# Attention, gated mixer and a Strassen-type MLP on one core: other pieces converted ahead, second tokens taken backwards

## The chip, the core and the metric

One NeuronCore of a Trainium2 chip runs the whole program. The metric is device time in microseconds (us) from the first to the last instruction and what lies around it, as the median of several runs. The kernel works in float32; matmuls take their operands as pairs of a high and a low part (`fp32r`), three matmuls for each product.

## The reference

Four sequences of 576 tokens go through attention (half of the heads local, half strided), then a gated mixer, then an MLP with a norm ahead of it. The change lies in the MLP:

```python
def _moe2_ref(x, g_ln, w_ch1, w_ch2):
    mu = np.mean(x, axis=-1, keepdims=True)
    var = np.mean((x - mu) ** 2, axis=-1, keepdims=True)
    xn = (x - mu) / np.sqrt(var + 1e-06) * g_ln
    ch = np.maximum(xn @ w_ch1, 0.0) @ w_ch2
    return (x + ch).astype(np.float32)
```

Here `x` has 4 x 576 x 512 values, `w_ch1` 512 x 2048, `w_ch2` 2048 x 512. Both weights arrive as 64-bit floats.

## The kernel before

**Stages.** Up to about 292 us attention and mixer run, batch after batch. Behind them stands `last_stage`, the MLP over three sets of 768 tokens (`sc` 0, 1, 2). `NW` is 8: the 2048 hidden units are eight *pairs* of two blocks of 128. A pair (`pair` for the first tokens, `joint_pair` for the second and third) multiplies by the scheme of Strassen and Winograd: seven products (`product`, L979, six matmuls each) in place of eight, with sums of weights and of inputs made ahead. For the first tokens the second product follows in plain form (`ch2`, L247 to L249). For the second and third tokens the second product is itself of the Strassen kind over the two sets: `step2` (L1197) with *slices* of `w_ch2` (M1 to M7) and *grains*, the inputs split in two parts (`grain`).

**Pieces of weights.** `wseq` counts pieces (i, j): j = 0, 1 are the two pieces of the first-product weight of pair i, j = 2, 3 those of the second-product weight. A raw piece is loaded as 64-bit numbers (512 KB, L784) into one of two raw buffers in `stg`, taken in turn, and turned into float32 by `from_f64` (one ScalarE instruction, L232; two of VectorE, L235 and L236). Ten pieces, listed in `PRE`, are converted in spare time before 292 us by `pre_w` in twenty halves and written to the scratch `w_d`; `piece` then loads them ready (256 KB, L779). `third` gives the float32 place of a second-product piece: two places in `stg`, one in the tile `late`. First-product pieces go to `stg2`.

`combine(i)` makes four sums in VectorE (L796 to L799), then splits all into the weight tile `w` of pair i (L760 on ScalarE, L761 on VectorE, or L218 and L219). `split_later` leaves the VectorE half to the next `flush`. `keep(i)` stores `w` to `w1_d` (L805); `fetch(i)` loads it again for later tokens (L814). There are two tiles for `w`, for even and odd i. `second(i)` splits the second-product pieces, and `store_f32` writes their float32 form to `w2_d` (L772), from where the slices come later.

**Order.** The first-token loop does `pair(0, i)`, then `prepare(6)`: six units of the list `units`, in which after pair i come the second weight of i + 1, `combine(i + 2)`, then the second-product pieces of i + 2, then the first-product pieces of i + 3. So `w` of pair i + 2 is made after pair i, and its pieces one pair earlier. All transfers go out from SyncE in one queue, which waits in order. A planner lays out each engine's order within what the data allows; `add_manual_dep` with `ORDER` fixes one instruction behind another.

**Second and third tokens.** `joint` runs pairs 0 to 7 of the second tokens, then M1 and M2 with i from 0 to 7, then pairs 0 to 7 of the third tokens, then M7, M6, M5, M4, M3. Weights 0 and 1 are fetched ahead of each set of pairs, and weight i + 2 after pair i. `sums_of(e)` makes four sums of blocks of `w_ch2` (L1136 to L1139), `store_sums` stores them, `sum_slices(m, places)` loads a sum and splits it for Mm. `rsqrt` makes the reciprocal root of the norm, half of the tokens at a time.

## Time and profile before

| what | us |
|---|---|
| median of 3 runs | 675.0 |
| lowest and highest run | 674.49, 679.81 |
| the profiled execution, whole | 677.46 |
| its span, first to last instruction | 675.5 |
| TensorE busy in the span | 651.6 |
| VectorE busy | 521.9 |
| ScalarE busy | 398.5 |

The granted clock of TensorE is 0.992 over the span, that is 2.4 GHz nearly throughout. In the profile PE is TensorE (PEld its weight loads), DVE VectorE, ACT ScalarE, POOL GpSimd and SP SyncE; L979 is line 979 of the kernel before. An idle time in brackets stands with the instruction that ended it and names what it had waited for. A tile's name is cut at its number (`w1b` stands for `w1b_0` and `w1b_1`), and every scratch tensor of weights is called `w_scratch`. TensorE's busy time overlaps from one matmul to the next; a pause can also be a missing record, and then no releaser stands behind it.

### The profile page before, as it was taken

To read this page: it belongs to the slowest core of one execution; us is meant where nothing else is said; L and a number is where in the kernel's file an instruction comes from. 1 tells how busy PE (TensorE), PEld (TensorE's weight loads), DVE (VectorE), ACT (ScalarE), POOL (GpSimd) and SP (SyncE) were. 2 spreads that over 40 slices of the span, in tenths; PEclk is the share of its full clock that TensorE was granted. 3 is DMA by queue.
4 is the path that set the end of the run, shared out by engine and by line. 5 is a ranking of instruction groups with operands and counts; after the bars stand their busy time and mean duration, and the time that the engine had idled before them with its cause. 6 is when DMAs were issued, how large, how long until landed. Compare 5 with 4: busy or idle time off the path is not lost.

```text
span 675.5 us, 12971 instructions
## 1 busy us (share of the span) xinstructions
PE 651.6 (96%) x4958; PEld 620.9 (92%) x4958; DVE 521.9 (77%) x997; ACT 398.5 (59%) x908; POOL 19.3 (3%) x24
## 2 busy tenths in 40 slices
PE   8989999999999999999999799999999999999997
PEld 6778989988897988999999699989999999999997
DVE  6878887585668688997699894585695774799893
ACT  5868967283458547645458863357874454856540
POOL 0021011000110011000000000000000000000000
PEclk9979999998999999999999999999999999999999
DMA  8772333457443470439978886498883797322234
GB/s 317 240 256 76 117 117 116 156 161 220 137 140 98 160 238 4 172 140 330 379 260 332 289 304 197 128 343 321 269 287 130 232 308 242 93 67 62 67 106 128
DMA packets 61453, 130.66 MB, mean 193 GB/s; under 512 B 5392, under 2 KB 28560, under 8 KB 60368
## 3 DMA queue, kind: packets, MB, share of 16 engines
q1 hardware_dynamic: 61392, 129.84, 57.6%
q8 instruction: 39, 0.64, 0.4%
q14 instruction: 22, 0.18, 0.1%
HBM read 94.69 MB, written 35.13 MB: 192 GB/s over the span
## 4 chain that ended last, share of the span: by engine, by line
PE 68%; DMA 10%; DVE 10%; ACT 8%; issue 2%; POOL 1%; SPq 0%; ACTq 0%; POOLq 0%; DVEq 0%
PE ps_p L979 18%; PE ps_m L1197 17%; PE ps_o L247 3%; PE ps_o L249 3%; PE ps_o L248 3%; DMA w_scratch<-w_p 2%; PE ps_y L249 2%; PE ps_y L247 2%; PE ps_y L248 2%; DMA stg<-in_w_ch 2%; PE ps_g L247 2%; PE ps_g L248 2%; PE ps_g L249 2%; PE ps_t L515 2%; PE ps_u L247 1%
## 5 line engine op out<-in xcount | busy, mean ns | idle before, releaser
L979 PE MATMUL ps_p<-x,w1b 128*128 128x384 f32 x672 | 120.6, 336 | 2.5 <-ACT u L1167 1.4
L979 PEld LDWEIGHTS ps_p<-x,w1b 128*128 128x128 f32 x672 | 116.1, 188 | 5.6 <-ACT u L1167 3.5
L1197 PE MATMUL ps_m<-t,w2c 128*128 128x384 f32 x420 | 74.1, 334 | 0.0
L1197 PEld LDWEIGHTS ps_m<-t,w2c 128*128 128x128 f32 x420 | 72.9, 188 | 0.0
L979 PE MATMUL ps_p<-x,w 128*128 128x384 f32 x336 | 63.5, 338 | 2.2 <-DVE w L219 1.3
L979 PEld LDWEIGHTS ps_p<-x,w 128*128 128x128 f32 x336 | 58.0, 188 | 4.2 <-DVE w L219 1.7
L247 PE MATMUL ps_u<-xhl,winl 128*128 128x288 f32 x128 | 39.2, 306 | 2.6 <-ACT u L354 2.6
L247 PE MATMUL ps_g<-wsg,vn 128*128 128x288 f32 x128 | 39.0, 305 | 0.0
L249 PE MATMUL ps_u<-xhl,winh 128*128 128x288 f32 x128 | 38.9, 304 | 0.0
L248 PE MATMUL ps_u<-xhl,winh 128*128 128x288 f32 x128 | 38.9, 304 | 0.0
L249 PE MATMUL ps_g<-wsg,vn 128*128 128x288 f32 x128 | 38.3, 299 | 0.0
L249 PE MATMUL ps_y<-gt,wout 128*128 128x288 f32 x128 | 38.1, 299 | 0.0
L248 PE MATMUL ps_g<-wsg,vn 128*128 128x288 f32 x128 | 38.1, 297 | 0.0
L247 PE MATMUL ps_y<-gt,wout 128*128 128x288 f32 x128 | 37.7, 297 | 0.0
L248 PE MATMUL ps_y<-gt,wout 128*128 128x288 f32 x128 | 37.6, 296 | 0.0
L248 PE MATMUL ps_o<-h,w2x 128*128 128x384 f32 x96 | 32.2, 335 | 0.2 <-DVE h L992 0.2
L249 PE MATMUL ps_o<-h,w2x 128*128 128x384 f32 x96 | 32.1, 334 | 0.0
L247 PEld LDWEIGHTS ps_u<-xhl,winl 128*128 128x128 f32 x128 | 25.2, 197 | 3.1 <-ACT u L354 2.7
L635 POOL TENSOR_TENSOR rs<-ve,neghalf 128x1 f32<-128x1 f32 x20 | 19.1, 957 | 244.5 <-DVE ve L633 244.5
L248 PEld LDWEIGHTS ps_u<-xhl,winh 128*128 128x128 f32 x128 | 25.2, 197 | 0.2
L249 PEld LDWEIGHTS ps_u<-xhl,winh 128*128 128x128 f32 x128 | 25.1, 196 | 0.0
L247 PEld LDWEIGHTS ps_g<-wsg,vn 128*128 128x128 f32 x128 | 24.1, 188 | 0.6
(340 smaller groups left out, 1670.3 us busy)
## 6 DMA issues: line engine op xcount, KB each, us to landing
w1b<-w_scratch SPq DMA_DIRECT2D x32, 512.0 KB, 4.8
w_scratch<-w SPq DMA_DIRECT2D x8, 1792.0 KB, 7.5
w1b<-w_scratch SPq DMA_DIRECT2D x48, 256.0 KB, 4.7
stg<-in_w_ch SPq DMA_DIRECT2D x22, 512.0 KB, 5.1
raw_p<-in_w_ch SPq DMA_DIRECT2D x20, 256.0 KB, 3.2
blk<-w_scratch SPq DMA_DIRECT2D x10, 512.0 KB, 5.4
qk<-in_qk_s SPq DMA_DIRECT2D x8, 601.0 KB, 4.8
qk<-in_qk_l SPq DMA_DIRECT2D x8, 592.0 KB, 4.9
```

Source lines behind the costliest of these rows:

```text
L247: nc.tensor.matmul(ps, lhsT=ll, rhs=rh, start=first, stop=False)
L248: nc.tensor.matmul(ps, lhsT=lh, rhs=rl, start=False, stop=False)
L249: last_mm[0] = nc.tensor.matmul(ps, lhsT=lh, rhs=rh, start=False, stop=last)
L515: nc.tensor.transpose(ps[:rows, (t - t0) * c:(t - t0 + 1) * c], src, ident)
L635: nc.gpsimd.tensor_tensor(out=rs, in0=ve, in1=neghalf[:, :1], op=ALU.pow)
L979: nc.tensor.matmul(o, lhsT=w[:, n0 + nk * k, a, :], rhs=x[:, c, k, :], start=first and k == 0 and n == 0, stop=k == 1 and n == 2, skip_gro ...
L1197: nc.tensor.matmul(banks[e, half][:, :TH], lhsT=sl[m, e][a][:, i, :], rhs=g[:, c, half * TH:(half + 1) * TH], skip_group_check=True, start ...
```

## The change

- `PRE` names other pieces: (2,0) and (2,1) stay; (3,0) to (6,1) of the first product are replaced by (3,2), (3,3), (4,2), (4,3), (5,2), (5,3), (6,2), (6,3) of the second. `ready` gives their place: the second-product ones go straight to `w2_d`, and `second` no longer puts them on the list that `store_f32` stores.
- The first-product pieces of pairs 3 to 6 are therefore raw. `wide(i)` gives their float32 place: the first 1792 columns of the second `late` tile for i = 3 and 5, `stg2` for the others. The third place of `third` moves to the last 512 columns of that tile. A `flush` stands ahead of the conversion of (7,0).
- One tile for even and one for odd weights serves all passes (`w1_tile`). The second tokens go through pairs 7 to 0, and M1 and M2 with i from 7 to 0. The two fetches ahead of the second and those ahead of the third tokens go.
- The roots of the second tokens are made at f = 9 and 12 of the first tokens' second half, not at pairs 6 and 7 of the second tokens.
- `sums_of` is put behind the last add of a pair, for e = 0 after pair 3 of the order (before: 2); `store_sums` follows after pair 4 (before: 3), in another order of blocks.
- The slices for M7 come in two steps: e = 0 after pair 5 of the third tokens into the two `w2y` tiles, e = 1 behind the last pair's `u4` copy. M7 takes i = 0, 1, 2 for e = 0, then the same for e = 1, then the rest.

```diff
@@ -73,7 +73,7 @@
           (2, "u", 0), (2, "u", 1), (2, "u", 3), (2, "u", 4), (2, "u", 5), (2, "u", 6), (2, "u", 7))
-PRE = (8, 9, 12, 13, 16, 17, 20, 21, 24, 25)
+PRE = (8, 9, 14, 15, 18, 19, 22, 23, 26, 27)
 XH_ACT = ((0, 1, 2, 3), ())
@@ -728,6 +728,9 @@
 
+    def ready(i, j):
+        return w_d[PRE.index(wseq.index((i, j)))] if j < 2 else w2_d[i, :, (j - 2) * WP:(j - 1) * WP]
+
     raws, stores = [], []
@@ -738,7 +741,7 @@
             n, half, f = stores.pop(0)
-            nc.sync.dma_start(out=w_d[n, :, half * (WP // 2):(half + 1) * (WP // 2)], in_=f)
+            nc.sync.dma_start(out=ready(*wseq[PRE[n]])[:, half * (WP // 2):(half + 1) * (WP // 2)], in_=f)
         if len(raws) > 1 or m >= 2 * len(PRE):
@@ -748,10 +751,15 @@
 
+    def wide(i):
+        if i not in (3, 5):
+            return big["stg2"]
+        return big["late", 1].rearrange("p f t -> p (f t)")[:, :1792].bitcast(U32)
+
     def third(n):
...
         if k == 2:
-            return big["late", 1].rearrange("p f t -> p (f t)")[:, 2 * TH:2 * TH + WP].bitcast(U32)
+            return big["late", 1].rearrange("p f t -> p (f t)")[:, 1792:].bitcast(U32)
         return big["stg"][:, 2048 + WP * k:2048 + WP * (k + 1)]
@@ -773,10 +781,12 @@
         stg = big["stg"]
-        w = third(2 * i + j - 2) if j > 1 else big["stg2"][:, WP * j:WP * (j + 1)]
+        w = third(2 * i + j - 2) if j > 1 else wide(i)[:, WP * j:WP * (j + 1)]
         k = wseq.index((i, j))
         if k in PRE:
-            nc.sync.dma_start(out=w.bitcast(F32), in_=w_d[PRE.index(k)])
+            nc.sync.dma_start(out=w.bitcast(F32), in_=ready(i, j))
+            if j == 2:
+                store_f32()
         else:
@@ -784,11 +794,13 @@
                 store_f32()
+            if (i, j) == (NW - 1, 0):
+                flush()
             from_f64(raw, w, None, 2)
...
     def combine(i):
-        c = big["stg2"].bitcast(F32)
+        c = wide(i).bitcast(F32)
         wf = c[:, 0:1024].rearrange("p (k f) -> p k f", k=KD)
@@ -798,17 +810,19 @@
         flush()
-        w = w1[i] = big["w1", i % 2].tile([P, 14, 2, P], F32R, tag="w1", name=f"w1_{i % 2}")
+        w = w1[i] = w1_tile(i % 2)
         (split_later if 0 < i < NW - 1 else split)(w[:, :, 0], w[:, :, 1], c.rearrange("p (n f) -> p n f", f=P))
...
 
+    def w1_tile(j):
+        if ("w1t", j) not in big:
+            big["w1t", j] = big["w1", j].tile([P, 14, 2, P], F32R, tag="w1", name=f"w1_{j}")
+        return big["w1t", j]
+
     def fetch(i):
-        j = i % 2
-        if ("w1b", j) not in big:
-            big["w1b", j] = big["w1", j].tile([P, 14, 2, P], F32R, tag="w1", name=f"w1b_{j}")
-        w = w1[i] = big["w1b", j]
+        w = w1[i] = w1_tile(i % 2)
         src = w1_d[i].rearrange("p (n a f) -> p n a f", a=2, n=14)
@@ -829,7 +843,8 @@
             (split_later if i + 1 < NW else split)(w2[i][0][:, k], w2[i][1][:, k], f)
-            f32s.append((i, k, f))
+            if wseq.index((i, 2 + k)) not in PRE:
+                f32s.append((i, k, f))
 
@@ -1082,14 +1097,14 @@
             leave(0, 0, d)
-        fetch(0)
-        fetch(1)
         for f in range(NF):
...
                 residual(0, 1)
+            if f in (9, 12):
+                rsqrt(1, f // 12)
             ch2(0, 1, f, 0)
@@ -1130,21 +1145,21 @@
 
-    def sums_of(e):
+    def sums_of(e, last):
         tt = nc.vector.tensor_tensor
         a11, a21, a22, a12 = (blk[g] for g in range(4))
-        tt(out=a22, in0=a21, in1=a22, op=ALU.add)
+        op = tt(out=a22, in0=a21, in1=a22, op=ALU.add)
+        tc.add_manual_dep(op.ins, last.ins.name, ORDER, reason="pair first")
         tt(out=a21, in0=a11, in1=a21, op=ALU.subtract)
...
     def store_sums(e):
-        for g in (1, 2, 0, 3):
+        for g in (3, 1, 2, 0):
             nc.sync.dma_start(out=ws_d[g, e], in_=blk[g])
 
-    def sum_slices(m, places):
-        n = NW * P
-        for e in range(2):
+    def sum_slices(m, places, behind=None, es=(0, 1)):
+        for e in es:
             hi, lo = places[2 * e:2 * e + 2]
@@ -1152,7 +1167,10 @@
                 nc.sync.dma_start(out=sl[m, e][1].bitcast(F32), in_=w2_d[:, :, c0:c0 + P].rearrange("i p q -> p i q"))
-            split(hi, lo, lo.bitcast(F32))
+            op = nc.scalar.activation(hi, lo.bitcast(F32), AF.Copy)
+            if behind is not None:
+                tc.add_manual_dep(op.ins, behind.ins.name, ORDER, reason="pair first")
+            nc.vector.tensor_tensor(out=lo, in0=lo.bitcast(F32), in1=hi, op=ALU.subtract)
 
@@ -1161,6 +1179,8 @@
         return a
+
+    pair_op, copy_op = [None], [None]
 
@@ -1179,13 +1199,13 @@
         u4 = tmp("u4")
-        copy(u4, a)
+        copy_op[0] = copy(u4, a)
         tt(out=b[:, 1, TH:], in0=o, in1=u4, op=ALU.add)
...
         product(sc, i, o, 4, False)
-        tt(out=b[:, 1, :TH], in0=o, in1=u2, op=ALU.add)
+        pair_op[0] = tt(out=b[:, 1, :TH], in0=o, in1=u2, op=ALU.add)
         relu(b[:, 1, :], b[:, 1, :])
@@ -1196,7 +1216,8 @@
                                      rhs=g[:, c, half * TH:(half + 1) * TH], skip_group_check=True,
-                                     start=m in (1, 2, 7, 4) and i == 0 and k == 0, stop=i == NW - 1 and k == 2)
+                                     start=(m, i) in ((1, NW - 1), (2, NW - 1), (7, 0), (4, 0)) and k == 0,
+                                     stop=i == (0 if m < 3 else NW - 1) and k == 2)
 
@@ -1252,39 +1273,36 @@
 
-        a = begin_pair(1, 0)
+        a = begin_pair(1, NW - 1)
         for i in range(NW):
-            a = joint_pair(1, i, a, hv[1, i], lambda: begin_pair(1, i + 1) if i + 1 < NW else None)
+            u = NW - 1 - i
+            a = joint_pair(1, u, a, hv[1, u], lambda: begin_pair(1, u - 1) if u else None)
             if i == 0:
...
                     load_block(0, g, g)
-            if i == 3:
+            if i == 4:
                 store_sums(0)
-            if i + 2 < NW:
-                fetch(i + 2)
+            if u > 1:
+                fetch(u - 2)
             for step in NORM2_AT.get(i, ()):
                 norm(2, step, 0)
-            if i == 2:
-                sums_of(0)
-            if i >= NW - 2:
-                rsqrt(1, i + 2 - NW)
-        fetch(0)
-        fetch(1)
+            if i == 3:
+                sums_of(0, pair_op[0])
         acc = {}
...
             acc[eh] = pl.tile([P, 512], F32, tag=tag, name="ps_m1")
-        order = [(m, i) for m in (1, 2) for i in range(NW)]
+        order = [(m, i) for m in (1, 2) for i in range(NW - 1, -1, -1)]
         ring[2] = big["wst"].tile([P, 2 * TC], F32R, tag="stg2", name="gr_3")
...
         for n, (m, i) in enumerate(order):
-            if (m, i) == (1, 2):
+            if (m, i) == (1, NW - 3):
                 for g in range(3):
                     load_block(1, g, g)
-            if (m, i) == (2, 0):
+            if (m, i) == (2, NW - 1):
                 other = {eh: bank_d("ps_m2") for eh in EH}
@@ -1292,8 +1310,8 @@
                 make(*order[n + len(ring)])
-            if (m, i) in EXPAND2_AT:
-                expand(2, EXPAND2_AT[m, i])
+            if (m, NW - 1 - i) in EXPAND2_AT:
+                expand(2, EXPAND2_AT[m, NW - 1 - i])
         for e, half in EH:
@@ -1318,7 +1336,7 @@
             if i == 2:
-                sums_of(1)
+                sums_of(1, pair_op[0])
             if i == 3:
@@ -1326,11 +1344,16 @@
                 rsqrt(2, i - 1)
+            if i == 4:
+                y0, y1 = (big["w2p", b].tile([P, NW * P], F32R, tag="w2y", name="w2c") for b in range(2))
+                sets = {0: [y1, y0]}
+            if i == 5:
+                sum_slices(7, sets[0], pair_op[0], (0,))
             if i == NW - 2:
-                sets = {}
-                sets[0] = slice_set(0)
-                sum_slices(7, sets[0])
-        sets[1] = slice_set(1)
+                free = thirds(0)
+                sets[0] += free[:2]
+        sum_slices(7, sets[0], copy_op[0], (1,))
+        sets[1] = free[2:] + thirds(1)
         sum_slices(6, sets[1])
@@ -1353,11 +1376,13 @@
             steps = [((0, 1), (0, 1), i) for i in range(NW)]
-            if m == 3:
+            if m == 7:
+                steps = [((e,), (0, 1), i) for e in range(2) for i in range(3)] + steps[3:]
+            elif m == 3:
                 steps = [(es, (half,), i) for es, half in (((0, 1), 0), ((0,), 1), ((1,), 1)) for i in range(NW)]
...
                 step2(m, i, banks, es, halves)
-                if n + 1 < len(ms):
+                if n + 1 < len(ms) and 1 in es:
                     grain(ms[n + 1], i, tags[i])
@@ -1380,11 +1405,10 @@
 
-    def slice_set(b):
+    def thirds(b):
         n = NW * P
         w = big["w1", b].tile([P, 2, 14, P], F32R, tag="w1", name="w2c").rearrange("p a b c -> p (a b c)")
-        y = big["w2p", b].tile([P, n], F32R, tag="w2y", name="w2c")
-        return [w[:, :n], w[:, n:2 * n], w[:, 2 * n:3 * n], y]
+        return [w[:, n * k:n * (k + 1)] for k in range(3)]
 
```

## Rows read from the trace of the kernel before

**Rows 1.** Page, busy time and share of the span of each engine, with instructions
```profile
PE 651.6 (96%) x4958; PEld 620.9 (92%) x4958; DVE 521.9 (77%) x997; ACT 398.5 (59%) x908; POOL 19.3 (3%) x24
```

**Rows 2.** Timeline, TensorE: start us, us, line, operation; in brackets idle before, releaser
```profile
333.02 1.31 PE L979 MATMUL ps_p<-x,w 128*128 128x384 f32 x6 [0.85 <-ACT s L1031]
...
381.91 0.98 PE L247 MATMUL ps_o<-h,w2y 128*128 128x384 f32 x4 [2.42 <-ACT h L989]
...
383.10 0.44 PE L248 MATMUL ps_o<-h,w2x 128*128 128x384 f32 x1 [0.20 <-DVE h L992]
...
386.11 4.43 PE L979 MATMUL ps_p<-x,w 128*128 128x384 f32 x24 [1.33 <-DVE w L219]
...
436.47 7.75 PE L979 MATMUL ps_p<-x,w1b 128*128 128x384 f32 x43 [0.41 <-ACT u L1167]
...
448.11 6.64 PE L979 MATMUL ps_p<-x,w1b 128*128 128x384 f32 x36 [0.95 <-DVE hb L1183]
...
454.99 1.34 PE L979 MATMUL ps_p<-x,w1b 128*128 128x384 f32 x6 [0.24 <-ACT u L1167]
...
585.84 1.31 PE L979 MATMUL ps_p<-x,w1b 128*128 128x384 f32 x6 [0.73 <-ACT u L1167]
```

**Rows 3.** Windows: length, busy us (instructions) of PE, PEld, DVE, ACT, POOL; clock, DMA share, GB/s
```profile
319.00:331.00 12.00, 12.00 (x71) 11.87 (x70) 8.87 (x16) 6.28 (x12) 0.00 (x0) 1.00 0.98 360
...
343.00:355.00 12.00, 12.00 (x71) 11.99 (x70) 11.97 (x21) 7.50 (x13) 0.00 (x0) 1.00 0.59 184
...
379.00:391.00 12.00, 8.04 (x43) 6.82 (x41) 11.96 (x23) 8.81 (x16) 0.00 (x0) 1.00 0.90 348
...
400.00:425.00 25.00, 25.00 (x147) 25.00 (x146) 15.44 (x26) 8.85 (x15) 0.00 (x0) 1.00 0.63 208
```

**Rows 4.** Chain that ended last, 292 to 400 us: start us, us, what
```profile
317.16 9.73 DMA stg<-in_w_ch
```

**Rows 5.** Timeline, SyncE issuing transfers in 312 to 320 us
```profile
314.26 1.44 SPq L772 DMA_DIRECT2D w_scratch<-late  x1
...
317.16 1.35 SPq L784 DMA_DIRECT2D stg<-in_w_ch  x1
```

**Rows 6.** Timeline, ScalarE, around the waits
```profile
310.21 0.47 ACT L1040 ACTIVATE u<-ps_p 128x384 f32<-128x384 f32 x1
...
327.00 0.66 ACT L232 ACTIVATE late<-stg 128x512 f32<-128x512 f32 x1 [1.38 <-DMA stg<-in_w_ch]
...
358.33 0.49 ACT L1040 ACTIVATE u<-ps_p 128x384 f32<-128x384 f32 x1
...
380.78 0.67 ACT L232 ACTIVATE stg<-stg 128x512 f32<-128x512 f32 x1 [1.21 <-DMA stg<-in_w_ch]
...
584.37 1.05 ACT L218 ACTIVATE w2c<-w2c 128x1024 fp32r<-128x1024 f32 x1
```

**Rows 7.** Timeline, VectorE, around the waits
```profile
328.16 0.69 DVE L236 SCALAR_TENSOR_TENSOR late<-stg,late 128x512 uint32<-128x512 uint32 x1
...
332.63 2.02 DVE L761 TENSOR_TENSOR w<-stg,w 128x1792 fp32r<-128x1792 f32 x1 [0.78 <-ACT w L760]
...
384.03 2.02 DVE L219 TENSOR_TENSOR w<-stg,w 128x1792 fp32r<-128x1792 f32 x1
...
445.90 1.23 DVE L1136 TENSOR_TENSOR blk<-blk,blk 128x1024 f32<-128x1024 f32 x1 [1.80 <-DMA blk<-w_scratch]
```

**Rows 8.** Transfers: landing of the raw loads of L784, then issues: count, KB each, median us to landing
```profile
DMA to landing us min/median/max: 3.4/5.1/13.5
...
w1b<-w_scratch SPq DMA_DIRECT2D x32, 512.0 KB, 4.8
...
w1b<-w_scratch SPq DMA_DIRECT2D x48, 256.0 KB, 4.7
...
w_scratch<-late SPq DMA_DIRECT2D x4, 256.0 KB, 8.4
```

## What the change will do to the time

> **What bounds the kernel now.** I read the page first: TensorE is busy for 96% of the span [rows 1], so nothing that only lightens another engine can show. What can be won is time in which TensorE stands still, and of that only what lies behind the first edited line that changes the order of work. The code before 292 us keeps its instructions (the twenty half pieces converted in spare time keep their sizes and places; sixteen of them come from another weight and go to another scratch tensor), so I take the stretch up to there as unchanged.
>
> Then I read TensorE's own timeline from 292 us on for rows that begin after a wait; the number in brackets is the wait and the name behind it what ended it [rows 2]. There are eight: 0.85 us at 333 us, 2.42, 0.20 and 1.33 us between 379 and 386 us, 0.41 us at 436 us, 0.95 and 0.24 us at 447 to 455 us, 0.73 us at 585 us: 7.13 us together, about 1.05% of 677.5 us. That is the ceiling of this change as long as no matmul is removed, and none is: pairs, steps and sums keep their matmuls, only their order turns. Nobody in this list waits directly for a transfer, so bytes saved are worth something only through the engine that does wait for them.
>
> What stands behind the waits? For the one at 333 us the chain of waits goes back to a raw load: issued at 317.16 us, under way for 9.73 us [rows 4]. ScalarE's timeline shows its conversion starting at 327.00 us after 1.38 us of waiting for that transfer [rows 6], and VectorE's shows the last write of the pair's first-product weight `w` ending at 332.63 + 2.02 = 334.65 us [rows 7]. ScalarE's copy of the PSUM bank, for which TensorE waited, came behind these. The three at 379 to 386 us have the same shape: ScalarE waits 1.21 us for a raw load (380.78 us), and the ReLU of pair 6 stands behind it; then the last pair's `w` is only done at 384.03 + 2.02 = 386.05 us, and TensorE starts 0.06 us later [rows 2, 6, 7]. VectorE is busy 11.96 of the 12 us of that window, TensorE 8.04 [rows 3].
>
> At 447 us VectorE has waited 1.80 us for a block of weights and then done the first of four sums, 1.23 us, ahead of the pair's own adds [rows 7]. At 585 us ScalarE splits a slice for 1.05 us just ahead of the copy `u` that TensorE needs [rows 6].
>
> **The change, part by part.** *Raw first-product weights.* Seven pairs of raw pieces are converted in the last stage before and after, so no conversion is removed. What moves: (3,0) and (3,1) are now raw and are fetched right behind (2,2) and (2,3); (6,2) and (6,3), which stood ahead of the last first-product pieces (7,0) and (7,1), become plain loads. So each weight `w` of pairs 3 to 6 now hangs on a raw load, and that of pair 7 gets its raw load one pair earlier, some 12 us (the copies `u` of pairs 1 and 5 start at 310.21 and 358.33 us, so a pair takes 48.1/4 = 12.0 us [rows 6]). The need for pair 7 was missed by 1.33 us and the queue that held up pair 6 loses two conversions; 12 us of lead covers both. The three waits are 2.42 + 0.20 + 1.33 = 3.95 us [rows 2]. Bounds: nothing comes back (0) or all of it (3.95). VectorE is full in that window [rows 3], so I keep 0.45 us as lost to it and take 3.5 us.
>
> The price is at pair 3. Raw buffer B comes free for (3,1) when it came free for (3,3) before, at 317.16 us [rows 5]. Raw loads land in 3.4 to 13.5 us, median 5.1 [rows 8]; the one in this place took 9.73 [rows 4], with the DMA engines busy 98% of 319 to 331 us [rows 3]. From the start of the conversion to the end of `w` the row chain is 327.00 to 334.65, 7.65 us [rows 6, 7]. So `w` of pair 3 is ready between 317.16 + 3.4 + 7.65 = 328.2 and 317.16 + 9.73 + 7.65 = 334.5 us, and TensorE comes to it at 333.02 - 0.85 = 332.2 us [rows 2]. New stall 0 to 2.3 us, against 0.85 now: between 0.85 won and 1.5 lost. The middle is 0.3 lost, which I take. In favour: the store of (3,2) and (3,3) behind that load is gone. Against: 512 KB more are read in this stretch. The two regions for `w` cost nothing; they spare SyncE the wait for the earlier split before it can fill one.
>
> A new wait on SyncE: the plain load of (3,3) into its place in `late` must wait until (2,2) is stored from there. That store is issued at 314.26 us [rows 5]; such stores take 8.4 us [rows 8], so SyncE is held to about 322.7 us, with (4,0), (4,1) and the keeping of pair 3's weight queued behind it. The raw buffers for these two come free at the earliest when the conversions of (3,0) and (3,1) end, 1.85 us from start to end (327.00 to 328.16 + 0.69) [rows 6, 7] after landing at 320.6 us or later: 322.4 us. So the wait costs at most 0.3 us that the buffers do not cost anyway, and I cost it at nothing.
>
> *Bytes.* Eight stores of 256 KB and four of the sixteen loads of `w1b` (512 and 256 KB parts, 1,792 KB each [rows 8]) go, 9.2 MB. From 343 us on the DMA share is 0.59 to 0.9 [rows 3] and no wait of TensorE hangs on the loads that go. I cost them at nothing; if this cover is wrong, it is a gain.
>
> *Second tokens in reverse.* The last two weights of the first pass are still on the core when the second begins, and the last two of the second when the third begins: this is what drops the four loads. Pairs and steps are only renumbered. The two reciprocal roots move to about 410 to 425 us; from 400 to 425 us VectorE is busy 15.4 and ScalarE 8.9 of 25 us [rows 3], so nothing.
>
> *Sums behind a pair.* The first of the four sums now follows the last add of pair 3 instead of running into pair 2. The block has had a whole pair more to land, so VectorE's 1.80 us wait and the 1.23 us ahead of the pair go, and with them 0.95 us of TensorE. The other three sums (1.2 us each) can still stand ahead of a copy: I leave the 0.24 us, and the 0.41 us at 436 us too, whose cause (splits of the plain slices) is untouched. Bounds 0 and 1.6 us; I take 0.95.
>
> *M7 in two steps.* Half of the slices come during pairs 5 and 6, the other half is split only behind the last `u` copy, and the first 18 matmuls use only the first half. The 1.05 us split no longer stands ahead of that copy: 0.73 us back [rows 2, 6]. The early split now costs 1.05 us of ScalarE inside pair 6, where it could cost the same again: bounds 0 and 0.73, I take 0.7.
>
> **Sum.** 3.5 - 0.3 + 0.95 + 0.7 = 4.85 us. The profiled execution took 677.46 us (span 675.5 and 1.96 around it) and would take 672.6; the median of the runs is 675.0, so I forecast 675.0 - 4.85 = 670.1 us, 0.7% less. With the bounds the sum runs from -1.5 to 7.1 us, 676.5 to 667.9.
>
> **Rivals.** *All pauses close.* ScalarE waited for both raw loads at the two costliest places [rows 6]; if the second-product pieces, now plain and half as large, free it there, the 0.85 at 333 us goes as well, and with the small ones the full 7.1 us: 667.9 us, or a little less if freed engines also smooth the short gaps below the list. Against: VectorE is at 11.96 of 12 us in two windows, 343 to 355 and 379 to 391 us [rows 3], and cannot give much.
>
> *The gain is given back early.* Pair 3 loses 1.5 us, pair 4 as much for the same reason, ScalarE's queue stands behind raw loads that are now needed sooner, and only the end is won: 3.95 - 3.0 and the later parts half, about 1.8 us, 673 us.
>
> *Raw loads set the pace (slower).* A raw buffer is free again after landing plus 1.85 us. Once the landing exceeds 12.0 - 1.85 = 10.2 us, each pair waits for its own weight. At the longest landing, 13.5 us [rows 8], each of pairs 3 to 6 is 13.5 + 1.85 - 12.0 = 3.3 us late, 13.4 us together, less the 4.85: 683.5 us. For it: the 9.73 us row is near the point. Against: the median of 5.1 us, and 0.59 DMA share right behind, from 343 us [rows 3]. The trace has ScalarE idle 1.38 us at the head of its queue for a raw load, with the copies that TensorE wants behind it [rows 6]. The Trainium skill's page "TensorE: Matmul & The Clock Gate", section "Architectural detail", says that ScalarE and VectorE are strictly first in, first out. By that rule a late raw load holds up PSUM copies even if its own weight is not yet needed, which speaks for this rival; the trace agrees, with 1.38 and 1.21 us.
>
> *No change at all.* If the order on ScalarE and VectorE is arranged anew so that other work takes the freed places, the sum is 0: 675 us; it is part of the second rival's share.
>
> **Chances.** About 1% is what a measurement of this kernel can tell from no change, 668.2 to 681.8 us. Forecast (668.3 to 672): 0.43. All pauses close (665 to 668.2): 0.32. Given back (672 to 677): 0.16. Raw loads set the pace: 0.09. So faster 0.32, same 0.59, slower 0.09. The range 665.0 to 676.5 holds the first three but for their edges.
>
> **What the changed profile would show.** No raw conversion between pair 6's products and pair 7's; TensorE without a pause of over 0.5 us where 379 to 386 us is now; at pair 3 a wait of TensorE for `w` of 0 to 2.3 us; VectorE's first sum not behind a DMA wait; no slice split between the last pair's copies; 12 loads of `w1b` in place of 16. I am wrong if TensorE waits for `w` at pairs 4, 5 and 6 as well, or if a new wait of VectorE at pair 6 or 7 takes the place of the old.

## The result and the profile after

The changed kernel takes 667.22 us (median of six runs, 664.72 to 668.62); the kernel before took 674.75 us beside it (six runs). The ratio is 0.9876, with 0.9835 to 0.9916 as its 95% interval: 7.5 us less, where 4.85 us were forecast, so 667.2 against 670.1. It lies inside the range of 665.0 to 676.5 and just on the other side of the line of 1% (668.2 us): the rival in which all pauses close named this time best.

The profiled execution of the changed kernel took 667.92 us, span 666.0. Its page, busy time of the engines (compare [rows 1]), and the two issues that stand for the weights loaded again (compare [rows 8]):

```profile
PE 648.0 (97%) x4958; PEld 618.6 (93%) x4958; DVE 521.7 (78%) x997; ACT 397.9 (60%) x908; POOL 19.3 (3%) x24
...
w<-w_scratch SPq DMA_DIRECT2D x24, 512.0 KB, 5.1
...
w<-w_scratch SPq DMA_DIRECT2D x36, 256.0 KB, 4.6
```

Every engine still has its instructions. There are 12 weight loads (24 and 36 parts) where [rows 8] had 16 (32 and 48). In the changed kernel these lines have moved: 979 is 994, 1167 is 1187, 784 is 794, 772 is 780, 779 is 787, 761 is 769, 989 is 1004; `w1b` is now called `w`.

I split the span at three points that both kernels have: the first matmul of the first MLP pair, the first product of the second tokens, and the first of the third. At the second and the third, some work of one part can run in the next, so the sum is safer than the single parts. The first point, before and after:

```profile
294.73 0.69 PE L979 MATMUL ps_p<-x,w 128*128 128x384 f32 x3
...
292.58 0.69 PE L994 MATMUL ps_p<-x,w 128*128 128x384 f32 x3
```

| us, profiled execution | before | after | less |
|---|---|---|---|
| from the start to the first MLP pair | 294.73 | 292.58 | 2.15 |
| first tokens | 138.57 | 131.95 | 6.62 |
| second tokens | 94.99 | 94.49 | 0.50 |
| third tokens to the last matmul | 143.14 | 142.93 | 0.21 |
| the three MLP parts together | 376.70 | 369.37 | 7.33 |

So in this pair of executions the gain lies in the first tokens. The 2.15 us ahead of them are no part of the change's work; the last section comes back to them. What is left on TensorE's timeline from 292 us on, in place of the eight rows of [rows 2]:

```profile
329.67 0.97 PE L247 MATMUL ps_o<-h,w2y 128*128 128x384 f32 x4 [1.08 <-ACT h L1004]
...
427.57 4.62 PE L994 MATMUL ps_p<-x,w 128*128 128x384 f32 x24 [0.28 <-ACT s L1187]
...
562.60 1.68 PE L994 MATMUL ps_p<-x,w 128*128 128x384 f32 x8 [0.53 <-ACT u L1187]
```

Three waits, 1.89 us, in place of eight with 7.13. The three waits before the last pair are gone, and so are those at 447, 455 and 585 us. None of the three that remain is for `w`. SyncE's raw loads of (7,0) and (7,1), before and after:

```profile
367.34 3.47 SPq L784 DMA_DIRECT2D stg<-in_w_ch  x2
...
354.74 2.42 SPq L794 DMA_DIRECT2D stg<-in_w_ch  x2
```

The list of waits says less than was won: 7.13 - 1.89 = 5.24 us, against 7.33. The number of matmuls in a window says more. Windows of before (length, busy us and instructions of PE, PEld, DVE, ACT, POOL; clock, DMA share, GB/s):

```profile
350.00:400.00 50.00, 46.00 (x255) 43.62 (x254) 46.08 (x79) 38.45 (x70) 0.00 (x0) 1.00 0.81 290
380.00:390.00 10.00, 6.55 (x34) 5.90 (x35) 10.00 (x19) 7.23 (x12) 0.00 (x0) 1.00 0.88 330
390.00:400.00 10.00, 9.96 (x55) 9.13 (x54) 9.71 (x17) 6.75 (x14) 0.00 (x0) 1.00 0.88 304
```

and of after:

```profile
350.00:400.00 50.00, 50.00 (x287) 49.22 (x286) 47.92 (x84) 38.07 (x69) 0.00 (x0) 1.00 0.57 208
380.00:390.00 10.00, 10.00 (x58) 9.74 (x57) 8.98 (x16) 9.31 (x19) 0.00 (x0) 1.00 0.22 65
```

In 350 to 400 us TensorE now issues 287 matmuls, before 255. At 50.00 / 287 = 0.174 us each, the 32 missing ones are 5.6 us, while the brackets of that stretch in [rows 2] add up to 3.95 us. Both windows show a clock of 1.00, so the clock is not the difference. From 390 to 400 us the kernel before has no bracket at all and a PE of 9.96 us, and yet 55 matmuls where ten microseconds of after hold 58. Busy time hides this, because a matmul's row is 0.33 us long while one starts every 0.17 us (two rows of before, where nothing waits):

```profile
419.60 0.33 PE L249 MATMUL ps_o<-h,w2x 128*128 128x384 f32 x1
419.77 0.33 PE L247 MATMUL ps_o<-h,w2y 128*128 128x384 f32 x1
```

A late start shortens the overlap first and shows as idle only when the overlap is used up.

### The profile page after: what moved, and what is told of

Its sections match the earlier page's. It is cut to its first block, busy times and chain, and to the rows that moved or that the text cites. A ratio compares the mean times of both kernels' runs of the same rounds, so it can differ in the third digit from the quotient of the medians.

```text
span 666.0 us, 12893 instructions
## 1 busy us (share of the span) xinstructions
PE 648.0 (97%) x4958; PEld 618.6 (93%) x4958; DVE 521.7 (78%) x997; ACT 397.9 (60%) x908; POOL 19.3 (3%) x24
## 4 chain that ended last, share of the span: by engine, by line
PE 79%; DMA 6%; ACT 6%; DVE 6%; issue 2%; POOL 1%; SPq 0%; ACTq 0%; POOLq 0%; DVEq 0%
PE ps_p L994 26%; PE ps_m L1217 17%; PE ps_o L247 3%; PE ps_o L249 3%; PE ps_o L248 3%; PE ps_y L249 2%; PE ps_y L247 2%; PE ps_y L248 2%; DMA w_scratch<-w_p 2%; PE ps_g L247 2%; PE ps_g L248 2%; PE ps_g L249 2%; DMA stg<-in_w_ch 2%; PE ps_t L515 1%; PE ps_u L247 1%
## 5 line engine op out<-in xcount | busy, mean ns | idle before, releaser
L994 PE MATMUL ps_p<-x,w 128*128 128x384 f32 x1008 | 182.8, 336 | 0.8 <-ACT u L1187 0.5
L994 PEld LDWEIGHTS ps_p<-x,w 128*128 128x128 f32 x1008 | 174.2, 188 | 4.8 <-ACT u L1187 2.0
L249 PE MATMUL ps_u<-xhl,winh 128*128 128x288 f32 x128 | 37.7, 295 | 0.0
L248 PE MATMUL ps_u<-xhl,winh 128*128 128x288 f32 x128 | 37.7, 294 | 0.0
L247 PEld LDWEIGHTS ps_g<-wsg,vn 128*128 128x128 f32 x128 | 24.1, 188 | 0.6
L717 DVE TENSOR_TENSOR y<-ps_y,x 128x288 f32<-128x288 f32 x32 | 14.4, 453 | 12.8 <-PE ps_y L249 12.0
L249 PEld LDWEIGHTS ps_g<-wsg,vn 128*128 128x128 f32 x128 | 24.0, 188 | 0.2
L248 PEld LDWEIGHTS ps_g<-wsg,vn 128*128 128x128 f32 x128 | 24.0, 188 | 0.1
L248 PEld LDWEIGHTS ps_u<-xhl,winh 128*128 128x128 f32 x128 | 24.0, 188 | 0.2
```

Source lines behind the costliest of these rows:

```text
L247: nc.tensor.matmul(ps, lhsT=ll, rhs=rh, start=first, stop=False)
L248: nc.tensor.matmul(ps, lhsT=lh, rhs=rl, start=False, stop=False)
L249: last_mm[0] = nc.tensor.matmul(ps, lhsT=lh, rhs=rh, start=False, stop=last)
L717: nc.vector.tensor_tensor(out=y[:, cs], in0=o, in1=x32[:, d, cs], op=ALU.add)
L994: nc.tensor.matmul(o, lhsT=w[:, n0 + nk * k, a, :], rhs=x[:, c, k, :], start=first and k == 0 and n == 0, stop=k == 1 and n == 2, skip_gro ...
```

## The experiments

For each of twelve kernels the time is the median with its ratio to the kernel before, which ran beside it (medians 673.2 to 674.7 us); "MLP" is the last row of the table above for its own profiled execution, one execution each. Of each edit the main lines are shown, with `...` for what is left out. Two traces of one and the same order of work differ by 0.5 us of the MLP (the run on the grain, below), so a size from two traces is good to about that.

### Which part carries the gain

**The change of pieces alone.** Of the change only `PRE`, `ready`, `wide`, the third place, the `flush` and the shorter list of stores; forward order, all fetches, sums and M7 as before.

```diff
-PRE = (8, 9, 12, 13, 16, 17, 20, 21, 24, 25)
+PRE = (8, 9, 14, 15, 18, 19, 22, 23, 26, 27)
...
-            f32s.append((i, k, f))
+            if wseq.index((i, 2 + k)) not in PRE:
+                f32s.append((i, k, f))
```

> The kernel before with the change of pieces alone (which pieces are converted ahead, the second region, the stores that fall away); tokens in the old order with all sixteen loads of weights, sums and slices as before. Queue theory (the gain comes from raw conversions that no longer stand ahead of pairs 6 and 7 on ScalarE and VectorE): the first tokens, from the first product of pair 0 to the last second product, take 138.6 us before and 132.0 in the changed kernel; here 132 to 133, the whole 5.5 to 6.5 us less than before, the waits of 436 to 455 us and 585 us still there. Traffic theory (the gain comes from loads that fall away and no longer crowd the DMA engines): the fetches that remain keep the end of the first tokens slow, 135 us or more, the whole at most 3 us less.

665.91 us, ratio 0.9876 (0.982 to 0.9933), the same ratio as the whole change; first tokens 132.07 us, MLP 370.32. TensorE's waits from the start of the MLP on:

```profile
326.09 0.97 PE L247 MATMUL ps_o<-h,w2y 128*128 128x384 f32 x4 [1.22 <-ACT h L1002]
...
424.13 8.11 PE L992 MATMUL ps_p<-x,w1b 128*128 128x384 f32 x44 [0.44 <-ACT s L1180]
...
573.59 1.31 PE L992 MATMUL ps_p<-x,w1b 128*128 128x384 f32 x6 [0.73 <-ACT u L1180]
```

The pauses before the last pair are gone. The 0.95 us of the sums are gone too, although the sums are still tied to nothing; the 0.73 us of M7 stand, as they should without that edit.

**Everything but the pieces.**

```diff
-PRE = (8, 9, 14, 15, 18, 19, 22, 23, 26, 27)
+PRE = (8, 9, 12, 13, 16, 17, 20, 21, 24, 25)
...
```

> The changed kernel with the old choice of pieces: tokens in reverse, twelve loads, roots, sums and slices as changed. Queue theory: the first tokens take 137 to 139 us again, TensorE waits 3 us or more ahead of pair 7's first product, the whole is 0.5 to 1.5 us less than before. Traffic theory: the four loads are gone, so the first tokens take 134 us or less and the whole is 4 us or more less.

671.04 us, ratio 0.9963 (0.9927 to 0.9998); first tokens 137.41 us, MLP 373.09. The profiled execution is the longest of its ten (677.94 us), and behind the first pause below its clock is at 0.50 from 385 to 388 us, which is in these two times. The pauses at the last pair are back:

```profile
385.06 1.65 PE L247 MATMUL ps_o<-h,w2y 128*128 128x384 f32 x4 [2.46 <-ACT h L991]
...
389.22 4.43 PE L981 MATMUL ps_p<-x,w 128*128 128x384 f32 x24 [0.45 <-DVE w L219]
```

The two halves do not add: alone, the pieces give 1.24% and the rest 0.4%, and together 1.24%. The pieces carry the gain; what the rest adds to them these medians can't tell from nothing (0.95 us of the MLP in the two traces, 370.32 against 369.37).

**Only the last pair's pieces exchanged.** (6,2) and (6,3) converted early, (6,0) and (6,1) raw; pairs 3 to 5 as before. This kernel lacks a `flush`, and the low half of pair 6's weight is then computed from values already overwritten; its time is to be read with that.

```diff
-PRE = (8, 9, 12, 13, 16, 17, 20, 21, 24, 25)
+PRE = (8, 9, 12, 13, 16, 17, 20, 21, 26, 27)
...
+            if j == 2:
+                store_f32()
```

> The kernel before with one pair of pieces exchanged: (6,2) and (6,3) are converted ahead in place of (6,0) and (6,1); nothing else. If the two raw pieces ahead of the last weight make the loss, most of the gain of the first tokens is here: 133 to 134.5 us in place of 138.6, the whole 4 to 5.5 us less than before. If the early stage needs the other six exchanges too (slack built up pair by pair), 136 us or more and the whole at most 2.5 us less.

676.79 us, ratio 1.0038 (1.0011 to 1.0066); first tokens 141.09 us. Slower than before, with a wait longer than any in [rows 2]:

```profile
373.40 6.12 PE L981 MATMUL ps_p<-x,w 128*128 128x384 f32 x24 [7.53 <-DVE w L761]
```

**The same with the `flush`.**

```diff
...
+            if (i, j) == (NW - 1, 0):
+                flush()
```

> The exchange of one pair of pieces of the third experiment again, now with the low half of pair 6's weight made ahead of the conversion of (7,0); in the third experiment it was made behind it, from overwritten data, and TensorE waited 7.5 us for it. If the two raw pieces ahead of the last weight are what costs the first tokens their time, they take 133 to 135 us and the waits of 379 to 386 us are gone, the whole 3 to 5.5 us less than before. If the other six exchanges are needed, the loss moves to pair 6 or 7 in another form: 137 us or more.

673.85 us, ratio 0.9994 (0.9969 to 1.0018): nothing won; first tokens 138.49 us. The timeline of TensorE, and of SyncE at pair 6's raw loads:

```profile
368.74 3.54 PE L983 MATMUL ps_p<-x,w 128*128 128x384 f32 x10 [5.39 <-DVE w L761]
...
348.75 4.02 SPq L786 DMA_DIRECT2D stg<-in_w_ch  x2
```

and windows around the pause:

```profile
364.00:365.00 1.00, 0.00 (x0) 0.00 (x0) 1.00 (x3) 1.00 (x3) 0.00 (x0) 1.00 0.44 127
...
371.00:372.00 1.00, 1.00 (x5) 1.00 (x4) 0.96 (x3) 0.99 (x2) 0.00 (x0) 0.50 1.10 459
...
374.00:375.00 1.00, 1.00 (x8) 1.00 (x7) 0.60 (x2) 1.00 (x1) 0.00 (x0) 1.00 0.48 148
```

The pause has moved one pair ahead, to pair 6, whose own `w` is now late. Its raw loads go out 59.0 us after the first MLP matmul (348.75 - 289.80). In the changed kernel, where (3,0) to (5,1) are raw as well and every raw load behind (3,1) stands earlier in the queue, the two for pair 6 go out at 344.60 us, 52.0 us after the first MLP matmul (292.58). So the gain at the last pair can't be had by exchanging that pair's pieces alone. That the other exchanges win it by bringing the whole chain of raw loads forward is argued from these times; the next run shows another way. The pause also costs more than its 5.4 us: behind it TensorE works at a clock of 0.50 for some us.

**No late raw pieces at all.** Twelve pieces converted early in place of ten, in four more half conversions, the last of them at 205.57 us; (6,2) and (6,3) are no longer raw, everything else is as before but for the same `flush` and store.

```diff
+          (2, "g", 1), (2, "g", 3))
...
-PRE = (8, 9, 12, 13, 16, 17, 20, 21, 24, 25)
+PRE = (8, 9, 12, 13, 16, 17, 20, 21, 24, 25, 26, 27)
```

> The kernel before with twelve pieces converted ahead in place of ten: (6,2) and (6,3) as well, nothing taken back. If the two raw conversions between pair 5 and the last weight cost the first tokens their time, the waits of 379 to 386 us (3.95 us) are gone, the first tokens take 133.5 to 135.5 us in place of 138.6 and the whole is 2.5 to 4.5 us less, unless the four more half pieces cost as much ahead of the last stage. If the loss sits in the whole chain of raw loads, it comes back at another pair and the first tokens take 137 us or more.

First tokens 131.62 us without one wait of TensorE: 7 us less than before, 0.3 less than the whole change and less than either expectation had it. So two raw conversions fewer ahead of the last pair do what the exchange of eight pieces does. Yet the whole takes 674.04 us, ratio 1.0002 (0.9971 to 1.0032): the MLP takes 370.90 us, 5.8 less than before, and the gain is lost ahead of it; the MLP starts at 296.27 us. Its trace shows where, at one place ahead of the MLP. TensorE's timeline, in the attention:

```profile
205.82 0.88 PE L424 MATMUL ps_sc<-qk 64*64 64x54 f32 x10 [3.30 <-DVE pt L446]
```

The chain that ended last, in 196 to 208 us (start us, us, what):

```profile
199.42 5.04 DMA w_scratch<-w_p
...
204.55 0.44 ACT w_p L233
```

Windows:

```profile
204.00:206.00 2.00, 0.18 (x4) 0.18 (x6) 0.99 (x3) 1.45 (x6) 0.00 (x0) 0.74 0.84 288
206.00:208.00 2.00, 1.28 (x29) 1.13 (x32) 2.00 (x7) 1.43 (x8) 0.00 (x0) 0.50 0.47 172
```

The store of a converted half took 5.04 us; ScalarE's next conversion waited for it (the buffer `w_p` is not free sooner), VectorE's half of the conversion waited for ScalarE, and behind it stood the work on `pt` for which TensorE waited 3.30 us, with the clock at 0.50 afterwards. That this one place makes up all of the lost 5.8 us isn't shown. The granted clocks of the ten runs go with it: 0.988 to 0.996, median 0.9915, where the runs of the kernel before beside them have a median of 0.995.

### The smaller parts

The intervals of all six kernels here overlap that of the changed one, so their medians do not separate these parts; where a size is given it comes from the MLP stretch of one trace each.

**Second tokens forward again,** with the four loads.

```diff
-        a = begin_pair(1, NW - 1)
+        a = begin_pair(1, 0)
...
+        fetch(0)
+        fetch(1)
```

> The changed kernel with second tokens and the steps of M1 and M2 in the old order and the four loads of weights back, issued where they were. Queue theory: bytes cost nothing, the first tokens take 132 us, the second 94.3 to 95, the whole as the changed kernel within 0.7 us. Traffic theory: the first tokens lose 2 us or more near their end, and the whole 2 to 4 us.

666.97 us, ratio 0.989 (0.9826 to 0.9954); MLP 369.57 against 369.37. The reverse order and its 7.2 MB (four times 1,792 KB) are worth nothing here.

**Sums without the tie,** at their old places.

```diff
-        op = tt(out=a22, in0=a21, in1=a22, op=ALU.add)
-        tc.add_manual_dep(op.ins, last.ins.name, ORDER, reason="pair first")
+        tt(out=a22, in0=a21, in1=a22, op=ALU.add)
...
-            if i == 3:
+            if i == 2:
                 sums_of(0, pair_op[0])
```

> The changed kernel with the sums of the second tokens and of the third not tied behind a pair's last add, the first after the third pair of the order and stored after the fourth, as before. If the tie is what took the 0.95 us wait away, the wait of TensorE behind the first sum is back, 0.5 to 1.2 us of it, the whole 0.5 to 1.3 us longer than the changed kernel. Rival: the blocks land earlier now that no weight loads stand ahead of them, so the wait stays away without the tie: no difference.

666.47 us, ratio 0.9885 (0.9855 to 0.9916); MLP 370.50. A wait is back, at another sum than in [rows 7], the first of those with e = 1 (TensorE, then VectorE):

```profile
484.28 2.60 PE L994 MATMUL ps_p<-x,w 128*128 128x384 f32 x12 [1.47 <-ACT u L1186]
...
480.47 1.23 DVE L1151 TENSOR_TENSOR blk<-blk,blk 128x1024 f32<-128x1024 f32 x1 [1.81 <-DMA blk<-w_scratch]
```

VectorE waits 1.81 us for a block and sums for 1.23 us, just ahead of the pair's work; with the tie no sum waits for a transfer. The gain is 1.1 us of the MLP, near the 0.95 forecast, though not at the pause that I had named: that one had gone with the pieces. The wait of 0.53 us at 562.60 us is gone here too; the run after the next comes back to it.

**M7 as before.**

```diff
...
-        sum_slices(7, sets[0], copy_op[0], (1,))
...
+                sets[0] = slice_set(0)
+                sum_slices(7, sets[0])
```

> The changed kernel with the slices for M7 as before: both halves asked for after pair 6, M7 in the old order of steps. If the two steps took the 0.73 us wait away, it is back in the last two pairs of the third tokens and the new 0.54 us wait at pair 5 is gone or not by its cause: the whole within 0.5 us of the changed kernel. If the 0.54 us wait comes from the early split, it is gone here.

667.98 us, ratio 0.9915 (0.9884 to 0.9945); third tokens 143.81 us against 142.93, 0.9 more.

```profile
562.60 1.68 PE L994 MATMUL ps_p<-x,w 128*128 128x384 f32 x8 [0.36 <-ACT u L1187]
...
577.40 1.31 PE L994 MATMUL ps_p<-x,w 128*128 128x384 f32 x6 [0.74 <-ACT u L1187]
```

The 0.74 us are back at the last copies. The smaller wait at 562.60 us is there without the early split too (0.36 here, 0.53 after), so the two steps did not make it.

**The grain of the next product one pair later.** ScalarE waits 1.22 us for a transfer at 557.57 us in the changed kernel, with a grain, ahead of that wait at 562.60 us.

```diff
-            if i == 5:
+            if i == 6:
```

> The changed kernel with the first grain of M7 made after pair 6 of the third tokens in place of pair 5. If the 0.54 us wait at pair 4 to 5 of the third tokens comes from that grain, which waits on ScalarE for the store of block 3 with the pair's copies behind it, it is gone and the third tokens take 142.0 to 142.4 in place of 142.9 us. Rival: the wait comes from the early split for M7, and stays.

666.35 us, ratio 0.9874 (0.9844 to 0.9903). TensorE still waits 0.65 us there (at 561.26 us). But the edit moved nothing: in the trace every engine has the changed kernel's instructions in the changed kernel's order. ScalarE's row of the grain, in the changed kernel and here:

```profile
557.57 0.85 ACT L218 ACTIVATE gr<-h 128x768 fp32r<-128x768 f32 x1 [1.22 <-DMA ws_scratch<-blk]
...
556.23 0.85 ACT L218 ACTIVATE gr<-h 128x768 fp32r<-128x768 f32 x1 [1.43 <-DMA ws_scratch<-blk]
```

The planner put it at the same place, still behind the store of a sum. So this run doesn't test the grain; it is the changed kernel a second time, with an MLP of 369.89 us against 369.37. The other traces test it in part: where the grain waits for that store 1.43, 1.35, 1.22, 1.18, 1.07, 1.04 and 0.96 us (this run, one region, the changed kernel, stores back, forward, M7 as before, and the last run below), TensorE waits 0.65, 0.65, 0.53, 0.50, 0.39, 0.36 and 0.28 us; where it waits 0.40 us (everything but the pieces) or not at all (before and five runs, that without the tie among them), TensorE doesn't stop there. That speaks for the late sums and their store, with the grain behind them, as the cause; no run moved the grain alone.

**One region for the weights,** `stg2` for every pair, with a `flush` ahead of each.

```diff
-        if i not in (3, 5):
+        if True:
             return big["stg2"]
...
-            if (i, j) == (NW - 1, 0):
+            if j == 0:
                 flush()
```

> The changed kernel with one region for the raw first-product weights of all pairs, flushed ahead of each first piece. If the second region is needed, the conversions of (3,0), (4,0), (5,0), (6,0) wait for the split before them, and TensorE waits for the weight at pairs 3 to 6: 1 to 3 us longer in the first tokens. If the raw loads are the late ones and not the place, 0 to 0.5 us.

668.62 us, ratio 0.9919 (0.9889 to 0.9948); first tokens 133.91 us, 2.0 more, MLP 371.52, 2.15 more. I had costed the two regions at nothing. The raw loads are not what is late: those of (7,0) and (7,1) go out at 352.62 us, 63.3 us after the first MLP matmul (289.37), against 62.2 in the changed kernel. Two of ScalarE's conversions are: those of (4,0) and (6,0) start 36.5 and 60.9 us after that matmul (325.85 and 350.24 us), against 33.0 and 59.5 (325.56 and 352.04). The waits of conversions for VectorE's half of the weight before, in 290 to 400 us, here and in the changed kernel (us in total, times, longest):

```profile
ACT stg L232 <- DVE w L769: 2.4, 3, 1.3
...
ACT stg L232 <- DVE w L769: 1.0, 1, 1.0
```

TensorE waits for no `w`, against the expectation; it waits for ScalarE's copies at 363.45 and 371.12 us (0.58 and 0.40 us), the wait of 1.08 us is gone, and the rest of the 2.0 us lies in delays without a bracket. That these come from the conversions is argued, not shown.

**The eight stores put back,** to a scratch tensor that nobody reads.

```diff
...
-            if wseq.index((i, 2 + k)) not in PRE:
-                f32s.append((i, k, f))
+            f32s.append((i, k, f))
```

> The changed kernel with eight stores of 256 KB more: the second-product pieces that come ready are stored once more, to a scratch tensor that nothing reads. Queue theory: SyncE is held at the places that the stores still read, and at most 1 us is lost, in the first tokens. Traffic theory: 2 MB more in the stretch with the fullest DMA engines cost 2 us or more.

667.13 us, ratio 0.9904 (0.9868 to 0.994); MLP 371.51, 2.14 more than after. The two ratios' intervals overlap, so the size rests on one trace. SyncE's waits in 290 to 400 us (line, what it waited for: us in total, times, longest):

```profile
SPq L788 <- DMA w_scratch<-stg: 10.3, 2, 5.8
...
SPq L788 <- DMA w_scratch<-late: 5.5, 2, 5.0
```

The timeline of SyncE at raw loads, and of TensorE:

```profile
329.52 1.30 SPq L795 DMA_DIRECT2D stg<-in_w_ch  x1
...
335.70 0.38 SPq L795 DMA_DIRECT2D stg<-in_w_ch  x1
...
362.94 3.36 PE L994 MATMUL ps_p<-x,w 128*128 128x384 f32 x18 [0.55 <-DVE w L770]
```

SyncE stands 10.3 and 5.5 us at plain loads (L788) whose place is still being stored from, and behind them stands a raw load: the two loads of one pair go out at 329.52 and 335.70 us, where the changed kernel issues them 1.4 us apart, from 331.71 us on (fence of the next section). TensorE then waits for a `w`, which in the changed kernel it never does. The size is nearer to what the traffic theory named (2 us or more; the first tokens alone take 135.60 us, 3.65 more). But the raw loads themselves do not take longer; landing of the six raw loads of pairs 5 to 7, here and in the changed kernel:

```profile
DMA to landing us min/median/max: 3.8/6.5/8.3
...
DMA to landing us min/median/max: 4.6/6.5/9.1
```

So the stores cost through the order of the queue: the raw loads go out later, not slower. The 7.2 MB of loads in the forward order cost nothing, but they go out from 368.9 us on, behind all raw loads.

### The wait that is left

In the changed kernel the wait at 329.67 us stands where [rows 2] have 0.85 us at 333.02. ScalarE around it, VectorE's last write of the weights of pairs 3 and 7, SyncE's raw loads for pairs 5 and 6:

```profile
325.56 0.66 ACT L232 ACTIVATE stg<-stg 128x512 f32<-128x512 f32 x1 [2.62 <-DMA stg<-in_w_ch]
328.53 0.67 ACT L232 ACTIVATE stg<-stg 128x512 f32<-128x512 f32 x1 [0.34 <-DMA stg<-in_w_ch]
329.11 0.51 ACT L1004 ACTIVATE h<-c 128x384 fp32r<-128x384 f32 x1
...
327.85 2.03 DVE L769 TENSOR_TENSOR w<-late,w 128x1792 fp32r<-128x1792 f32 x1
...
371.69 2.03 DVE L219 TENSOR_TENSOR w<-stg,w 128x1792 fp32r<-128x1792 f32 x1 [0.83 <-ACT w L218]
...
331.71 2.65 SPq L794 DMA_DIRECT2D stg<-in_w_ch  x2
...
344.60 1.82 SPq L794 DMA_DIRECT2D stg<-in_w_ch  x2
```

ScalarE stands 2.62 us at the head of its queue for a raw piece of pair 4, needed only a pair later; the split of pair 3's weight, a copy, the second raw piece and then the ReLU `h` that TensorE wants come behind it. The Trainium skill's page "TensorE: Matmul & The Clock Gate", section "Architectural detail", says that ScalarE and VectorE are strictly first in, first out; this row agrees, with 2.62 us of waiting ahead of work that was needed sooner.

**Asking for these two conversions later:** two units fewer after pair 1, two more after pair 2.

```diff
-                prepare(len(units[done[0]:]) if i + 3 == NW else 6)
+                prepare(len(units[done[0]:]) if i + 3 == NW else {1: 4, 2: 8}.get(i, 6))
```

> The changed kernel with pieces (4,0) and (4,1) asked for after pair 2 in place of after pair 1, so that their conversions stand behind more of pair 2's work on ScalarE. If the 1.08 us wait at pair 2 comes from these conversions standing at the head of ScalarE's queue (2.62 and 0.34 us for their loads) with the ReLU behind them, it is gone and the first tokens take 130.5 to 131.2 us, unless the weight of pair 4 is now late: then TensorE waits for it at pair 4, 0.5 to 2 us.

671.28 us, ratio 0.9927 (0.9899 to 0.9955); first tokens 135.40 us, 3.4 more, which neither branch of the expectation named. The wait at 329.67 us is gone, and four others have come in; two of them:

```profile
374.31 1.32 PE L994 MATMUL ps_p<-x,w 128*128 128x384 f32 x6 [0.47 <-ACT u L1055]
...
379.47 0.44 PE L933 MATMUL ps_m<-sr,one 128*128 128x384 f32 x1 [0.66 <-DVE sr L910]
```

That the wait went with these conversions agrees with the cause; the four new ones stand behind pair 2, which now has eight units to hide, though that they come from there was not tried by itself. None of the twelve kernels beats the changed one by more than its interval.

## Why the prediction was right or wrong, point by point

- **The last pair (3.5 us): right in mechanism, too small.** The raw loads of (7,0) and (7,1) went out 72.6 us after the first MLP matmul (367.34 - 294.73) and go out after 62.2 now (354.74 - 292.58): 10.4 us earlier, against the 12 worked out. The weight is done at 371.69 + 2.03 = 373.72 us with TensorE busy throughout. The pieces alone took 6.5 us off the first tokens. The mis-sized thing is the sum of 3.95 us, which I took from brackets and called a ceiling; the number of matmuls puts the same stretch at 5.6 us. The 0.45 us that I held back for a full VectorE were not lost either: VectorE is busy 47.92 of 50 us in 350 to 400 us, and TensorE does not stop.
- **Pair 3 (0.3 us lost; bounds 0.85 won to 1.5 lost): within the bounds.** Its weight is done at 327.85 + 2.03 = 329.88 us, which on the clock of before is 332.0 (2.15 us later), between the 328.2 and 334.5 given and just ahead of the 332.2 at which TensorE came. TensorE did not wait for it. The 0.85 us nevertheless stayed, as 1.08, with another cause than [rows 4] gave: not a second-product piece but ScalarE waiting for pair 4's.
- **Two regions, and eight stores, at nothing: wrong.** For the stores the step that failed is "no wait of TensorE hangs on the loads that go. I cost them at nothing": it asked for bytes and for direct waits, not for what stands behind a store in SyncE's queue. In one trace each, the second region is worth 2.15 us of the MLP and the missing stores 2.14 us; the stores hold SyncE ahead of raw loads, the single region holds ScalarE's conversions behind VectorE's splits. I had used the store only as a point in favour of pair 3, and had named a spared wait of SyncE for the region without a price. The two sizes are no parts of a sum: each is what the changed kernel loses without that one thing.
- **Four loads fewer and reverse order, at nothing: right,** 0.2 us of the MLP.
- **Sums (0.95 us): near in size, wrong in place.** The pause at 447 us went with the pieces alone; the tie is worth 1.1 us of one trace, against a pause of 1.47 us that would otherwise come at 484 us. It seems to cost the 0.53 us at 562.60 us.
- **M7 (0.7 us): right** as far as one trace tells, 0.9 us. The early split did not cost it back.
- **The signs named.** No pause at the last pair, no `w` waited for at pair 3, no sum behind a transfer, no pause at the last copies and 12 loads: all came. One did not: two raw conversions still lie between pairs 6 and 7 (373.59 and 374.75 us, the second-product pieces of pair 7), only nobody waits for them. The 0.41 us at 436 us, which I left standing, is 0.28 at 427.57 us.
- **The rivals.** *Raw loads set the pace* asked for landings over 10.2 us; those of the changed kernel have 5.5 us as their median and 9.1 as their longest, and TensorE waits for no `w`. A pair that waits for its own `w` came only in the exchanges of one pair (5.39 us with `flush`), and there its two raw loads landed in 6.1 and 5.5 us: they went out late, they did not land late. *Given back early* happened only as the 1.08 us. *All pauses close* came nearest, though by another road: 1.89 us of pauses stayed, and the short delays below the list, which I had mentioned in half a sentence, made up for them.
- **The sum (4.85 us).** The MLP gave 7.33 us with the clock at 1.00 in both profiles, so the forecast had the direction and the place, and two thirds of the size. That the medians differ by as much, 7.5 us, is partly luck: they hold a share of the granted clock (last section) that was no term of the sum.

## What to carry to other kernels

Count the instructions of the bounding engine in a window and compare with a stretch that runs free; the sum of its listed waits understates what the waits cost, so it is no ceiling. Before costing a removed transfer by its bytes, ask what stands behind it in its issuing queue: here 7.2 MB of loads behind all raw loads cost nothing, and 2 MB of stores that later loads had to wait for cost about 2 us. When a late conversion holds up a pair, moving only that pair's load can move the pause one pair ahead, as here; the loads ahead of it in the queue have to come earlier too, or a conversion has to go. And look in the trace whether an edit of the program's order has moved the instruction at all.

## What the runs showed of the hardware that was not expected

A pause of TensorE costs more than its bracket, in two ways. From start to start, the four pauses of before in the first tokens took 1.02, 2.59, 0.37 and 1.50 us beyond the usual 0.17 us for each matmul, where [rows 2] list 0.85, 2.42, 0.20 and 1.33: 0.17 us more each. The matmul right behind the pause is 0.44 us long, and the next starts 0.28 us after it, 0.11 more again (383.10 in [rows 2], and the row behind it):

```profile
383.38 0.34 PE L249 MATMUL ps_o<-h,w2x 128*128 128x384 f32 x1
```

So a pause costs its bracket and 0.28 us. The eight of before and the three of after all show it: five times 0.28 us and the 5.24 us of brackets are 6.6 of the 7.33 us; the rest are delays too short for a bracket. And behind some pauses the granted clock is down: in the exchange with `flush`, TensorE stood still for 5.39 us, then ran at 0.50 (1.2 GHz), with 5 matmuls in the window of one microsecond at 371 us, until it was back at 1.00 (2.4 GHz) with 8 in the one at 374 us. Behind 2.46 us in the run with everything but the pieces it was at 0.50 too, behind the 2.42 us of before it stayed at 1.00.

The 2.15 us ahead of the MLP belong here: the profile of before has a mean clock of 0.93 in its first 50 us and 0.97 in 150 to 200 us, that of after 1.00 in both, with the same instructions in the same order on every engine up to there but for their sources and places of store. The start of the MLP lay anywhere from 288.86 to 298.98 us in the fourteen profiles. In the four profiles with a clock below 1.00 in the first 50 us, TensorE has just waited 1.67 to 2.72 us for ScalarE's `u` at about 44 us; in the ten others that wait is 1.03 to 1.89 us. Why one execution gets such a wait and dip and another does not stays open. The medians hold some of it: four of the changed kernel's six runs have a mean clock of 0.999 or 1.00, but only three of the sixty runs of the kernel before beside the experiments. The windows of before:

```profile
0.00:50.00 50.00, 43.99 (x508) 36.16 (x509) 39.22 (x90) 32.93 (x78) 3.78 (x7) 0.93 0.79 272
...
150.00:200.00 50.00, 48.54 (x410) 45.23 (x409) 30.49 (x80) 23.95 (x63) 4.61 (x5) 0.97 0.56 169
```
